# Sums of weight blocks for the seven-product chunks: made between the attention heads and fetched, instead of made in the last stretch

## The chip, the cores and the metric

One core of one Trainium2 chip runs the whole program. The metric is device time in microseconds (us). The kernel before has a median of 1070.12 us over three runs (1069.92 to 1073.11). A difference of about 0.3% is what a measurement of this kernel can tell from none.

## What is computed

Block-causal attention for 8 batches of 8 heads (576 positions, head width 64), then a feed-forward layer on the 4608 tokens of 512 features, with a hidden width of 2048:

```python
scores = 0.125 * q @ k.T                       # per head, 576 x 576
scores = where(row // 64 >= col // 64, scores, -1e9)
attn = exp(scores - max) / (sum + 1e-9)
x = (attn @ v)                                 # heads side by side: 4608 x 512
h = x @ w_in                                   # 512 x 2048
g = maximum(0.01 * h, h)
out = g @ w_out                                # 2048 x 512
```

Everything is float32. For TensorE each matrix of the feed-forward layer is split into a rounded high part and a low part (what is left after rounding), and a product is made of three: high by high, high by low, low by high.

## The kernel before

**Stages.** The 64 heads are worked through one after another. The first 14 turn their probabilities on TensorE; the other 50 turn them with VectorE transposes (L795) and two trips through DRAM (`way`, `turn`). The tokens make 18 chunks of 256. Twelve of them go through the plain feed-forward code, `ffn1` (L894) and `ffn2` (L921), whose matmuls stand between those of the heads and behind them. The last six chunks go through `tail()` as three pairs, and the tail is what the change is about.

**The tail.** A pair of chunks is multiplied with seven block products where eight would be needed: each matrix is cut into 2 by 2 blocks, sums and differences of blocks are multiplied, and the results are combined. For each of the eight units `u` of the hidden width, `first8` (L1092) makes seven products of `x` and `w_in` blocks with six matmuls each, VectorE combines them out of PSUM (L1105), ScalarE applies the leaky ramp (L1108), and the result is stored to DRAM in `gd` through four staging buffers, two for even and two for odd units. When the three pairs are through, `second8` (L1221) reads `gd` back and makes seven products with `w_out` blocks in 24 steps.

**The weight sums.** The seven products need sums of weight blocks, high part plus low part, added and subtracted in a fixed way. `combos(u)` makes those of `w_in`: one operation on 128x512 and six on 128x256 into scratch (`xin` for the first seven units, the unused `x8` for the eighth), then a split of the four results into high and low parts in `sum8[u]` and in place of one weight block. This lies ahead of the first pair. `combos2(u)` makes those of `w_out`: two operations on 128x512 and four on 128x256 in the scratch `x8`, a split of one result over a weight block, and a store of the other three to DRAM in `td`. These eight pieces stand among the products of `first8`, at the places listed in `SUMS`. `combos3(u)` fetches `td` into `sum8[u]` once `first8` of the third pair is done with unit `u`, and splits it. The additions go through `op2`, which offers each to VectorE (L965) and to GpSimd (L966).

**What sets the order.** `Plan` walks through a model of the five engines and writes one fixed order per engine; each operation has a rank (its due place, in heads, or from 1000 on in the tail) and a choice of engines with costs. Operations of VectorE named `DVE+` and all of GpSimd are not planned to run at the same time; those named `DVE` may run beside GpSimd. The plan only sets orders: at run time nothing keeps the two engines apart. All DMAs are issued by SyncE in one order, so an issue that waits holds back those behind it. `split_x` and `splits8` split the inputs; `inputs8` loads a pair's inputs into `x8` (1024 KB).

Of the kernel before, what the change touches and what calls it, by code (L numbers as in the profile page):

```python
# [9 lines left out]
F32 = mybir.dt.float32  # L10
# [26 lines left out]
RL = -2.684  # L37
# [14 lines left out]
SUMS = [1, 2, 4, 10, 11, 12, 14, 19]  # L52
EARLY = 7
RL8 = -6.0
RT8 = -1.0
RM = 11.035
# [3 lines left out]
RS = -16.177  # L60
RG = -8.8
OFF1 = 3.882
# [11 lines left out]
FILLTO = -153.36  # L74
# [206 lines left out]
def attention_ffn(ctx: ExitStack, tc: tile.TileContext, q2: bass.AP, k2: bass.AP, qk: bass.AP, v: bass.AP, w_in: bass.AP, w_out: bass.AP, out: bass.AP):  # L281
# [84 lines left out]
    td = fixed([P, 3 * CH], F32, "td", NU, dram)  # L366
# [416 lines left out]
    def turn(i, row, pkeys):  # L783
# [22 lines left out]
        flipped(0, 13, 14, 1, 0, 0, 64)  # L806
        for y, (a0, a1, b0, b1) in enumerate(((0, 1, 1, 4), (1, 3, 0, 4), (3, 4, 0, 3))):
# [131 lines left out]

    def tail():  # L940
        if not TAIL:
            return
# [9 lines left out]
        old += [("xh", 1, e) for e in cells]  # L952
# [8 lines left out]

        def op2(n, dst, one, two, plus, rank, reads, writes, by=None):
            name = "tensor_add" if plus else "tensor_sub"
            both = [
                ("DVE", dve2(n), lambda: getattr(nc.vector, name)(dst(), one(), two())),  # L965
                ("POOL", pool2(n), lambda: getattr(nc.gpsimd, name)(dst(), one(), two())),  # L966
            ]
            add(both[1:] if by == "POOL" else both, rank, reads, writes)
# [17 lines left out]

        def combos(u, rank):
            w0, w1 = wkeys[("wi", u)], wkeys[("wi", u + NU)]
            s0, s1 = [("S", u, 0)], [("S", u, 1)]
            heap, keys = (flat8, x8s) if u >= EARLY else (raw8, xins)  # L990
            at = lambda y, n=1: heap()[:, y * CH : (y + n) * CH]
            four = lambda ap: ap.rearrange("p (d f) -> p d f", f=P)
            op2(WIDE, lambda: four(at(1, 2)), lambda: f32(sides(u, 0)), lambda: f32(sides(u, 1)), True, rank, w0, keys)
            for h in range(2):
                op2(
                    CH, lambda h=h: four(at(3 * h)), lambda h=h: f32(sides(u + NU, 0)[:, 2 * h : 2 * h + 2]),
                    lambda h=h: f32(sides(u + NU, 1)[:, 2 * h : 2 * h + 2]), True, rank, w1, keys,
                )
            op2(CH, lambda: at(3), lambda: at(0), lambda: at(3), True, rank, [], keys)
            op2(CH, lambda: at(0), lambda: at(1), lambda: at(0), False, rank, [], keys)  # L1000
            op2(CH, lambda: at(1), lambda: at(3), lambda: at(1), False, rank, [], keys)
            op2(CH, lambda: at(2), lambda: at(2), lambda: at(1), False, rank, [], keys)
            split(3 * CH, lambda: sum8(u, 0), lambda: sum8(u, 1), lambda: at(1, 3), rank, keys, s0, s1)
            split(
                CH, lambda: sides(u + NU, 0)[:, 0:2], lambda: sides(u + NU, 1)[:, 0:2], lambda: four(at(0)), rank, keys,
                [x for x in w1 if not x[1]], [x for x in w1 if x[1]],
            )

        def combos2(u, rank):
            w0, w1 = wkeys[("wo", u)], wkeys[("wo", u + NU)]  # L1010
            base = 4 * (u % 2)
            at = lambda y, n=1: flat8()[:, (base + y) * CH : (base + y + n) * CH]
            d8 = 2 * (u % 2)
            c0, c1, c2, c3 = (in8(d8 + d, d8 + d + 1, h * CH, (h + 1) * CH) for d in range(2) for h in range(2))
            for y, (f, w) in enumerate(((u, w0), (u + NU, w1))):
                op2(WIDE, lambda y=y: at(2 * y, 2), lambda f=f: f32(woh[:, f]), lambda f=f: f32(wol[:, f]), True, rank, w, (c2 + c3) if y else (c0 + c1))
            op2(CH, lambda: at(0), lambda: at(1), lambda: at(0), False, rank, c1, c0)
            op2(CH, lambda: at(1), lambda: at(3), lambda: at(1), False, rank, c3, c1)
            op2(CH, lambda: at(3), lambda: at(3), lambda: at(0), False, rank, c0, c3)
            op2(CH, lambda: at(2), lambda: at(3), lambda: at(2), False, rank, c3, c2)  # L1020
            split(
                CH, lambda: woh[:, u, CH:], lambda: wol[:, u, CH:], lambda: at(0), rank, c0,
                [x for x in w0 if not x[1]], [x for x in w0 if x[1]],
            )
            add([("SP", ISSUE, lambda: nc.sync.dma_start(td[u], at(1, 3)))], rank, c1 + c2 + c3, [("td", u)], lag="gs")

        def combos3(u, rank):
            s0, s1 = ("S", u, 0), ("S", u, 1)
# [328 lines left out]
```

## Time and profile before

| | us |
|---|---|
| median of three runs (lowest, highest) | 1070.12 (1069.92, 1073.11) |
| profiled execution, its own time | 1071.98 |
| its span in the trace | 1070.2 |
| TensorE busy | 1027.7 |
| VectorE busy | 798.8 |
| ScalarE busy | 610.5 |
| GpSimd busy | 420.1 |

The table of stretches gives the busy time of each engine in a window; where TensorE's busy time equals the window, it never stood still for longer than its pipeline hides. The table of waits names, for the engine's idle time, who ended it. A matmul's duration in the trace contains its pipeline, so matmuls overlap and their mean durations don't add up to busy time. In the tables `x` is the tile `x8`, `sum` is `sum8`, `more` and `piles` and the upper half of `xin` are the staging buffers, `p_s`, `p_v`, `p_h`, `p_o` are PSUM tiles, and `big` and `new` hold the split inputs.

### The profile page before, as it was taken

What the parts mean: (1) busy time and instruction counts of PE and PEld (TensorE: products, weight loads), DVE (VectorE), ACT (ScalarE), POOL (GpSimd) and SP (SyncE); (2) the same over time, 40 slices, a digit from 0 to 9 for tenths busy, and PEclk for the clock granted to TensorE, in tenths of its full rate; (3) what the DMA queues carried; (4) which work ended last, traced back from release to release, by engine and by line L of the source; (5) the groups of instructions that cost most, each with busy time, mean ns of one, the idle gap of its engine ahead of it and who ended that gap; (6) DMA issues with size and microseconds to landing.
All of it is one profiled execution on the core that took longest, in us unless ns stands there. A gap on an engine that the chain in (4) does not pass through costs nothing. (4 is left out here: it accounts for less than half of the span.)

```text
span 1070.2 us, 21248 instructions
## 1 busy us (share of the span) xinstructions
PE 1027.7 (96%) x7336; PEld 910.8 (85%) x7336; DVE 798.8 (75%) x1932; ACT 610.5 (57%) x1437; POOL 420.1 (39%) x413
## 2 busy tenths in 40 slices
PE   7979999999999999999999999999999789889998
PEld 4658889888888888888888888888999789879998
DVE  7887978688778787878768778760998767578664
ACT  7778768576766665666756656651443434434332
POOL 3344227253343444345433423421435534155331
PEclk9999999999999999999999999999999999999999
DMA  6554534676776576786766865574005466665442
GB/s 202 164 185 137 167 106 132 208 211 178 222 207 211 182 224 179 216 242 173 231 200 201 226 177 178 169 232 118 21 10 169 139 206 182 190 194 172 150 155 72
DMA packets 131228, 185.80 MB, mean 174 GB/s; under 512 B 14896, under 2 KB 103728, under 8 KB 131120
## 3 DMA queue, kind: packets, MB, share of 16 engines
q1 hardware_dynamic: 131120, 184.44, 57.3%
q8 instruction: 58, 0.95, 0.4%
q14 instruction: 50, 0.41, 0.1%
HBM read 107.68 MB, written 76.71 MB: 172 GB/s over the span
## 5 line engine op out<-in xcount | busy, mean ns | idle before, releaser
L894 PE MATMUL p_h<-big,wih 128*128 128x256 f32 x1216 | 246.7, 281 | 0.0
L921 PE MATMUL p_o<-woh,big 128*128 128x512 f32 x768 | 236.8, 395 | 0.0
L894 PEld LDWEIGHTS p_h<-big,wih 128*128 128x128 f32 x1216 | 200.0, 189 | 10.0 <-issue 2.2
L312 POOL TENSOR_TENSOR big<-piles,big 128x512 fp32r<-128x512 f32 x80 | 106.3, 1329 | 204.0 <-ACT big L297 169.6
L795 DVE STREAM_TRANSPOSE turn<-prow 128x128 f32<-128x128 f32 (+3 forms) x400 | 144.8, 396 | 21.5 <-POOL prow L630 5.4
L921 PEld LDWEIGHTS p_o<-woh,big 128*128 128x128 f32 x768 | 133.3, 188 | 21.4 <-issue 2.4
L630 POOL TENSOR_SCALAR prow<-prow,nmrec 128x448 f32<-128x448 f32 (+4 forms) x98 | 60.3, 621 | 176.0 <-DVE nmrec L617 134.3
L894 PE MATMUL p_h<-big,wil 128*128 128x256 f32 x448 | 123.4, 280 | 0.0
L921 PE MATMUL p_o<-wol,big 128*128 128x512 f32 x384 | 119.7, 393 | 0.0
L909 ACT ACTIVATE piles<-p_h 128x512 f32<-128x512 f32 x96 | 57.2, 596 | 87.9 <-PE p_h L894 83.3
L600 ACT ACTIVATE prow<-p_s,nmrec 128x448 f32<-128x448 f32 (+4 forms) x150 | 83.1, 559 | 32.3 <-DVE nmrec L591 27.1
L894 PE MATMUL p_h<-xh,wih 128*128 128x256 f32 x320 | 87.8, 280 | 0.0
L894 PE MATMUL p_h<-xh,wil 128*128 128x256 f32 x320 | 87.3, 278 | 0.0
L921 PEld LDWEIGHTS p_o<-wol,big 128*128 128x128 f32 x384 | 72.2, 188 | 15.7
L894 PEld LDWEIGHTS p_h<-big,wil 128*128 128x128 f32 x448 | 85.2, 190 | 0.3
L600 ACT ACTIVATE prow<-p_v,nmrec 128x576 f32<-128x576 f32 (+1 forms) x150 | 71.4, 484 | 19.1 <-DVE nmrec L591 18.5
L312 POOL TENSOR_TENSOR ks<-qk_in,ks 64x576 fp32r<-64x576 f32 x52 | 74.5, 1433 | 5.1 <-DMA turn<-way 1.5
L710 PE MATMUL p_v<-turn,vt 128*64 128x256 f32 (+3 forms) x700 | 75.7, 368 | 0.0
L591 DVE TENSOR_REDUCE nmrec<-p_s 128x1 f32<-128x448 f32 (+4 forms) x150 | 72.0, 518 | 1.1
L710 PEld LDWEIGHTS p_v<-turn,vt 128*64 128x64 f32 x700 | 44.5, 137 | 28.6 <-issue 17.9
L632 ACT ACTIVATE prow<-prow,nmrec 128x320 f32<-128x320 f32 (+4 forms) x113 | 59.0, 536 | 12.4 <-DVE nmrec L617 12.1
L297 ACT CAST ks<-qk_in 64x576 fp32r<-64x576 f32 x63 | 42.3, 671 | 36.7 <-PE p_v L570 30.7
(281 smaller groups left out, 2376.5 us busy)
## 6 DMA issues: line engine op xcount, KB each, us to landing
way<-turn SPq DMA_DIRECT2D x50, 448.0 KB, 3.8
way<-turn SPq DMA_DIRECT2D x100, 168.0 KB, 3.5
turn<-way SPq DMA_DIRECT2D x100, 168.0 KB, 3.6
qk_in<-in_qk SPq DMA_DIRECT2D x50, 288.0 KB, 3.8
turn<-way SPq DMA_DIRECT2D x100, 112.0 KB, 3.6
out<-piles SPq DMA_DIRECT2D x36, 256.0 KB, 3.4
raw<-in_w_in SPq DMA_DIRECT2D x16, 512.0 KB, 4.0
raw<-in_w_out SPq DMA_DIRECT2D x16, 512.0 KB, 3.7
```

Source lines behind the costliest of these rows:

```text
L297: one = lambda: nc.scalar.copy(dst(), src())
L312: ("POOL", pool2(n), lambda: nc.gpsimd.tensor_sub(dst(), one(), two())),
L591: [("DVE", dve(kw[t]), lambda t=t, ap=ap, flat=flat: nc.vector.tensor_reduce(nm[z][: qn[t], at_col[t] : at_col[t] + 1], ap[: qn[t]], axis= ...
L600: nc.scalar.activation(o, ap[: qn[t]], AF.Exp, bias=nm[z][: qn[t], at_col[t] : at_col[t] + 1], scale=1.0, accum_out=sums[z][: qn[t], at_co ...
L630: ("POOL", pool1(kw[t]), lambda: nc.gpsimd.tensor_scalar(p(), p(), by, 1.0, op0=ALU.mult, op1=ALU.mult)),
L632: ("ACT", act(kw[t], True) + 108, lambda: nc.scalar.mul(p(), p(), by)),
L710: nc.tensor.matmul(dst, later["vt"][z][:, j], src, start=start, stop=stop)
L795: nc.vector.transpose(dst, src.rearrange("p (s b i) -> p s b i", b=4, i=32))
L894: nc.tensor.matmul(p_h[z][:, i, :], w[:, d, f * P : (f + 1) * P], (xl if x else xh[y])[:, d, :], start=first and k == 0 and (u > 0 or i == ...
L909: add([("ACT", act(512), lambda: nc.scalar.activation(g, p_h[z], AF.Prelu, alpha=0.01))], rank, [("h", z)], ["g"])
L921: nc.tensor.matmul(p_o[m], a[:, i, m * P : (m + 1) * P], w[:, u + NU * i, :], start=u == 0 and k == 0, stop=u == NU - 1 and k == 5,)
```

## The change

The sums of `w_in` and of `w_out` are both made by a new function, `sums_ahead`, in 16 pieces (two for each unit) with ranks 22.0, 24.136, and so on to 54.04, that is, among the heads from the 23rd on. Each piece waits for the transposes of the head of its rank. The scratch is `xr`, which held the first batch's attention output until the third plain chunk had read it; it is cut in two halves, one for `w_in` pieces and one for `w_out` pieces. All additions of these pieces are given to VectorE (`PREBY`). At the end of each piece SyncE stores four results (512 KB) to DRAM in `td`, which grows from three to eight blocks for each unit. In the tail, `brought` takes the place of the additions: it loads one block or three blocks from `td` into the low part's place, ScalarE or VectorE rounds them into the high part's, and a subtraction leaves the low part. `op2`'s VectorE choice is now named `DVE+`. The pace of three plain chunks, and numbers that place loads, the splits and the trips through DRAM, are changed too.

```diff
-RL = -2.684
+RL = -2.305
-RX = -0.204
+RX = -0.49
-PACE = [5.0, 5.0, 5.67, 4.14, 5.0, 5.0, 4.52, 5.0, 5.0, 5.0, 5.0, 5.17, 5.0, 5.0, 5.0, 5.0, 6.28, 4.59]
+PACE = [5.0, 5.0, 5.67, 4.14, 5.46, 5.0, 4.52, 5.0, 5.55, 5.39, 5.0, 5.17, 5.0, 5.0, 5.0, 5.0, 6.28, 4.59]
-SUMS = [1, 2, 4, 10, 11, 12, 14, 19]
-EARLY = 7
+SUM0 = 2
+RC8 = -8.0
+PRE0 = 22.0
+PRE1 = 2.136
+PREBY = "DVE"
...
+    def sums_ahead():
+        spare = [("spare", y, c) for y in range(2) for c in range(4)]
+        add([("POOL", 1, lambda: None)], 0, [], [("x", 0, h, y) for h in range(H) for y in range(2)] + spare)
...
+            rank = PRE0 + PRE1 * j
+            gate = [("head", min(int(rank), NH - 1))]
...
+                sum_of(WIDE, lambda: four(at(1, 2)), lambda: side(u, 0), lambda: side(u, 1), True, rank, w0 + gate, k1 + k2)
...
+                sum_of(CH, lambda: at(2), lambda: at(3), lambda: at(2), False, rank, k3, k2)
+            add([("SP", ISSUE, lambda: nc.sync.dma_start(td[u][:, y], at(0, 4)))], rank, k0 + k1 + k2 + k3, [("td", u, y)], lag="pre")
...
-                ("DVE", dve2(n), lambda: getattr(nc.vector, name)(dst(), one(), two())),
+            ("DVE+", dve2(n), lambda: getattr(nc.vector, name)(dst(), one(), two())),
...
+        def brought(u, y, rank, part, top, low, tops, lows):
+            a, e = (0, 1) if part else (1, 4)
+            src = lambda: td[u][:, y, a * CH : e * CH]
...
+            add([("SP", ISSUE, lambda: nc.sync.dma_start(f32(low()), shape(src())))], rank + RC8, [("td", u, y)], lows, lag="in1" if part else "in3")
+            n = (e - a) * CH
+            casting(n, top, lambda: f32(low()), rank, lows, tops)
+            op2(n, low, lambda: f32(low()), lambda: f32(top()), False, rank, tops, lows)
```

Up to the first of the new additions the orders of VectorE and TensorE are those of before, row by row apart from buffer numbers: VectorE's first 493 rows and TensorE's first 1151. From there they differ. Three places show how.

VectorE among the heads, about the 37th head, in the changed kernel: `nmrec` and `prow` are the heads' maxima and probabilities, `turn` the transposed ones, `xr` the scratch of the sums.

```order
L594 TENSOR_REDUCE nmrec<-p_s 128x1 x2
L798 STREAM_TRANSPOSE turn_1489<-prow_0_111 64x4x32
L947 TENSOR_TENSOR xr<-woh,wol 128x512
L544 SCALAR_TENSOR_TENSOR qs_1471<-qk_in,qs_1471 64x576
L619 TENSOR_REDUCE nmrec<-sums 128x3
L620 RECIPROCAL nmrec<-nmrec 128x3
L947 TENSOR_TENSOR xr<-woh,wol 128x512
L634 TENSOR_SCALAR prow_1_112<-prow_1_112,nmrec 128x192
L634 TENSOR_SCALAR prow_0_111<-prow_0_111,nmrec 64x64
L947 TENSOR_TENSOR xr<-xr 128x256
L619 TENSOR_REDUCE nmrec<-sums 128x2
```

The additions stand one by one between the steps of the heads, all on VectorE; before, nothing of `xr` or of the weights stood there.

VectorE in the tail, where the third unit of the first pair is combined, in the kernel before:

```order
L1105 TENSOR_TENSOR xin<-more,p_h_689 128x2x128
L965 TENSOR_TENSOR x_8058<-x_8058 128x256
L1105 TENSOR_TENSOR xin<-xin,p_h_690 128x2x128
L965 TENSOR_TENSOR x_8058<-x_8058 128x256
L1105 TENSOR_TENSOR xin<-xin,p_o_100 128x2x128
L965 TENSOR_TENSOR x_8058<-x_8058 128x256
L965 TENSOR_TENSOR wol<-x_8058,woh 128x256
L965 TENSOR_TENSOR x_8058<-x_8058 128x256
L1105 TENSOR_TENSOR more<-more,p_h_690 128x2x128
L1105 TENSOR_TENSOR piles<-piles,p_s 128x2x128
L965 TENSOR_TENSOR x_8058<-x_8058 128x256
```

And in the changed kernel, from the second unit of the first pair on:

```order
L947 TENSOR_TENSOR x_8287<-x_8287 128x2x256
L1123 TENSOR_TENSOR piles<-piles,p_s 128x2x128
L947 TENSOR_TENSOR xin<-x_8287 128x512
L1123 TENSOR_TENSOR more<-more,p_v 128x2x128
L1123 TENSOR_TENSOR xin<-more,p_h_689 128x2x128
L1123 TENSOR_TENSOR xin<-xin,p_h_690 128x2x128
L1123 TENSOR_TENSOR xin<-xin,p_o_100 128x2x128
L1123 TENSOR_TENSOR more<-more,p_h_690 128x2x128
L1123 TENSOR_TENSOR piles<-piles,p_s 128x2x128 x2
L1123 TENSOR_TENSOR piles<-piles,p_v 128x2x128 x3
```

The combining steps now follow each other; the two differences of the next pair's inputs (`x`, `xin`) stand behind the 9th combining step of the pair, where before they stood behind the 33rd, since `x8` is no longer scratch.

SyncE's issues at the end of the first pair's stores (`gd_80`) and the start of the second pair's (`gd_81`), in the changed kernel:

```order
L1155 DMA gd_80<-more 128x2x128
L1155 DMA gd_80<-piles 128x4x128 x2
L1155 DMA gd_80<-more 128x2x128
L1059 DMA x_8287<-xt_97 128x4x512
L1155 DMA gd_81<-more 128x4x128
L1155 DMA gd_81<-xin 128x4x128
L1155 DMA gd_81<-more 128x2x128
L1155 DMA gd_81<-piles 128x4x128 x2
```

Before, the third pair's load of inputs (the row with `xt`) stood among the stores of the second pair's fourth unit, and eight stores to `td` stood among the `gd` stores of the three pairs; now the load opens the second pair and no store to `td` is among them.

SyncE among the heads in the changed kernel, at the store of one piece:

```order
L815 DMA way_72<-turn_1492 32x1344
L986 DMA td_87<-xr 128x1024
L531 DMA qk_in<-in_qk 128x576
L827 DMA turn_1492<-way_72 32x3x448
L827 DMA turn_1492<-way_72 32x448
```

The new store stands ahead of the next head's inputs and of a trip back from DRAM.

## Rows read from the trace of the kernel before

**Rows 1.** The page's first part: busy us, share of the span, instructions

```profile
PE 1027.7 (96%) x7336; PEld 910.8 (85%) x7336; DVE 798.8 (75%) x1932; ACT 610.5 (57%) x1437; POOL 420.1 (39%) x413
```

**Rows 2.** Stretches of the whole: length, busy us (instructions) by engine, clock, DMA share, GB/s

```profile
0.00:50.00 50.00, 40.44 (x260) 29.29 (x261) 38.59 (x113) 37.68 (x104) 19.79 (x36) 1.00 0.64 195
50.00:100.00 50.00, 43.89 (x295) 33.27 (x294) 41.13 (x104) 38.83 (x101) 20.26 (x16) 0.93 0.49 147
...
233.00:496.00 263.00, 263.00 (x1823) 228.65 (x1822) 206.06 (x583) 171.89 (x432) 108.17 (x108) 1.00 0.69 202
...
711.00:800.00 89.00, 89.00 (x589) 78.52 (x588) 53.90 (x100) 33.00 (x63) 27.23 (x20) 1.00 0.23 69
```

**Rows 3.** Stretches of the tail's first products, 800 to 941, same columns

```profile
840.00:860.00 20.00, 15.41 (x121) 14.33 (x120) 18.44 (x28) 8.01 (x20) 16.14 (x14) 1.00 0.45 144
...
sum 141.00, PE 123.45 PEld 119.29 DVE 100.52 ACT 56.24 POOL 60.46; mean PE 17.64 PEld 17.04 DVE 14.36 ACT 8.04 POOL 8.64
```

**Rows 4.** Waits of TensorE, 800 to 941: total us, times, longest us

```profile
PE p_v L1092 <- DVE piles L1105: 4.0, 3, 2.0
PE p_v L1092 <- DVE more L1105: 2.4, 2, 1.9
PE p_v L1221 <- ACT piles L1108: 2.1, 1, 2.1
PE p_h L1092 <- DVE piles L1105: 1.7, 1, 1.7
PE p_h L1092 <- DVE big L965: 1.3, 1, 1.3
PE p_s L1092 <- ACT piles L1108: 1.2, 1, 1.2
PE p_v L1092 <- ACT piles L297: 1.2, 1, 1.2
```

**Rows 5.** Additions in scratch, 800 to 941, by shape: busy us, mean ns, idle before

```profile
L965 DVE TENSOR_TENSOR x<-x 128x256 f32<-128x256 f32 x28 | 19.2, 687 | 0.0
L965 DVE TENSOR_TENSOR x<-woh,wol 128x512 f32<-128x512 f32 x6 | 6.4, 1072 | 1.0 <-DMA td<-x 1.0
L965 DVE TENSOR_TENSOR x<-wih,wil 128x256 f32<-128x256 f32 x2 | 0.8, 419 | 0.0
L965 DVE TENSOR_TENSOR x<-wih,wil 128x512 f32<-128x512 f32 x1 | 0.7, 684 | 0.0
...
L966 POOL TENSOR_TENSOR x<-woh,wol 128x512 f32<-128x512 f32 x10 | 15.8, 1591 | 2.8 <-DMA td<-x 2.0 <-DVE big L965 0.6
L966 POOL TENSOR_TENSOR x<-x 128x256 f32<-128x256 f32 x11 | 9.3, 844 | 5.4 <-DMA x<-gd 3.4 <-DVE x L965 1.7
```

**Rows 6.** Line 965 between 750 and 800: duration ns min/median/max, first and last start

```profile
L965 DVE TENSOR_TENSOR xin<-xin x27: 424/426/1398, 752.7 to 792.0; 128x256 f32<-128x256 f32 x27
```

**Rows 7.** DMA issues by tile, 800 to 941: times, KB each, median us to landing

```profile
gd<-piles SPq DMA_DIRECT2D x23, 256.0 KB, 2.5
...
x<-xt SPq DMA_DIRECT2D x1, 1024.0 KB, 8.9
```

**Rows 8.** ScalarE's instructions around 838, 875, 882: start, us, [idle before <- releaser]

```profile
837.87 0.37 ACT L297 COPY piles<-p_v 128x256 f32<-128x256 f32 x1 [4.39 <-DMA gd<-piles]
...
874.66 0.37 ACT L297 COPY piles<-p_s 128x256 f32<-128x256 f32 x1 [1.44 <-DMA gd<-piles]
...
881.86 0.37 ACT L297 COPY more<-p_o 128x256 f32<-128x256 f32 x1 [3.50 <-DMA gd<-more]
```

**Rows 9.** VectorE's transposes of heads 22 (first) and 55 (last): start, us

```profile
232.63 0.90 DVE L795 STREAM_TRANSPOSE turn<-prow 128x384 f32<-128x384 f32 x2 [0.70 <-POOL prow L630]
...
495.38 0.77 DVE L795 STREAM_TRANSPOSE turn<-prow 128x384 f32<-128x384 f32 x2 [0.17 <-ACT prow L632]
```

**Rows 10.** GpSimd's subtractions for the plain chunks, 233 to 496, and VectorE's longest wait there

```profile
L312 POOL TENSOR_TENSOR big<-piles,big 128x512 fp32r<-128x512 f32 x32 | 42.2, 1319 | 76.3 <-ACT big L297 59.7 <-DVE big L298 15.3 <-POOL prow L630 0.8
...
DVE p_v L318 <- PE p_v L570: 18.1, 19, 2.4
```

**Rows 11.** The heads' last matmuls on `turn`: duration ns, first and last start us

```profile
L710 PE MATMUL p_v<-turn,vt x56: 272/327/644, 720.5 to 738.7; 128*64 128x128 f32 x16, 128*64 128x256 f32 x16, 128*64 128x192 f32 x16, 128*64 128x512 f32 x8
```

More of the change, by code (lines that the diff above doesn't have):

```diff
@@ L806, in turn @@
         flipped(0, 13, 14, 1, 0, 0, 64)
+        plan.writer["head", i] = plan.writer["turn", x, 0, 0]
         for y, (a0, a1, b0, b1) in enumerate(((0, 1, 1, 4), (1, 3, 0, 4), (3, 4, 0, 3))):
@@ L938, in ffn2, with op2 @@
                 add([("SP", ISSUE, store)], rank, [key], [("out", c, m)], lag="out")
+    def op2(n, dst, one, two, plus, rank, reads, writes, by=None):
+        name = "tensor_add" if plus else "tensor_sub"
+        both = [
+            ("DVE+", dve2(n), lambda: getattr(nc.vector, name)(dst(), one(), two())),
+            ("POOL", pool2(n), lambda: getattr(nc.gpsimd, name)(dst(), one(), two())),
+        ]
+        add(both[1:] if by == "POOL" else both[:1] if by == "DVE" else both, rank, reads, writes)
@@ L951, in tail @@
         old += [("x", 0, h, y) for h in range(H) for y in range(2)] + [("xs", d, y) for d in range(2) for y in range(2)]
-        old += [("xh", 1, e) for e in cells]
+        old += [("xh", 1, e) for e in cells] + [("spare", y, c) for y in range(2) for c in range(4)]
         in8 = lambda d0=0, d1=ND, e0=0, e1=2 * CH: [("x8", d, e) for d in range(d0, d1) for e in range(e0, e1, BLK)]
@@ L985, in sum8 @@
             return later["sum8"][u][:, low].rearrange("p a b -> p (a b)")
-        def combos(u, rank):
[L988 to L1005, printed above, removed]
@@ L1009, in combos2 @@
         def combos2(u, rank):
[L1010 to L1025, printed above, removed]
-        def combos3(u, rank):
-            s0, s1 = ("S", u, 0), ("S", u, 1)
-            add([("SP", ISSUE, lambda: nc.sync.dma_start(f32(sum8(u, 1)), td[u]))], rank, [("td", u)], [s1], lag="gs")
-            rank = max(rank, TR + 8 * TAIL + u // 2 + RT8)
-            casting(3 * CH, lambda: sum8(u, 0), lambda: f32(sum8(u, 1)), rank, [s1], [s0])
-            op2(3 * CH, lambda: sum8(u, 1), lambda: f32(sum8(u, 1)), lambda: f32(sum8(u, 0)), False, rank, [s0], [s1])
+            w0 = wkeys[("wo", u)]
+            brought(u, 1, rank, 1, lambda: woh[:, u, CH:], lambda: wol[:, u, CH:], [x for x in w0 if not x[1]], [x for x in w0 if x[1]])
+        def combos3(u, rank):
+            brought(u, 1, rank, 0, lambda: sum8(u, 0), lambda: sum8(u, 1), [("S", u, 0)], [("S", u, 1)])
         def inputs8(k, rank):
@@ L1271, in tail @@
                 first8(k, u, TR + 8 * k + u)
-                for y in range(NU):
-                    if int(SUMS[y]) == 8 * k + u:
-                        combos2(y, TR + SUMS[y])
+                y = 8 * k + u - SUM0
+                if y >= 0 and y % 2 == 0 and y // 2 < NU:
+                    combos2(y // 2, TR + 8 * k + u)
                 if k == TAIL - 1:
-                    combos3(u, TR + 8 * k + u)
+                    combos3(u, TR + 8 * TAIL + u // 2 + RT8)
         for n in range(8 * TAIL):
@@ L1319, in attention_ffn @@
                 ffn2(c, u, rank + rate[c] * LAG / NU + 0.003)
-    tail()
+    if TAIL:
+        sums_ahead()
+        tail()
     if FILL:
```

58 lines of the change are left out of this document (40 added, 18 removed), and 2 rows, old and new, of the table MOVES.

## The prediction

> **What bounds the kernel now.** I read the busy times first [rows 1]: TensorE is busy 96% of the span, the next engine, VectorE, 75%. The average hides the stages, so the stretches come next [rows 2]. From 0 to 100 us TensorE is idle for 9.6 + 6.1 = 15.7 us while the program starts. From 233 to 496 it is busy for all 263 us, and for all 89 us from 711 to 800: TensorE alone sets the time there, and work on other engines is free as long as TensorE finds its operands. In the tail's first products, 800 to 941, it is busy 123.45 of 141 us [rows 3]: 17.5 us are lost, most densely between 840 and 860, where VectorE is busy 18.44 of 20 us and GpSimd 16.14. TensorE's waits there [rows 4] name the releasers: the seven rows make 13.9 us, the other seven of that table, each 0.8 or less, make 3.6. Nearly all wait for VectorE to empty a PSUM bank (L1105) or for ScalarE.
>
> I sort the 17.5 us by their roots. ScalarE's copies into the staging buffers at 838, 875 and 882 stand behind stores to `gd` that have not landed [rows 8]. A store of 256 KB lands in 2.5 us in the median, but the 1024 KB load of the next pair's inputs, issued on the same queue, takes 8.9 us [rows 7], and the stores behind it share its time. The waits of 1.2 us (L297), of 2.0 (the longest of the first row) and of 1.7 fall at these copies: **4.9 us come from DMA**. Of what VectorE released (4.0 + 2.4 + 1.7 + 1.3 and 2.9 of the small ones = 12.3) the other **8.6 us come from VectorE being late**, since additions in the scratch stand between its combining steps. The remaining 4.0 us, among them 2.1 for the first step of `second8`, wait for ScalarE.
>
> **What the change removes.** The additions of rows 5 go: 19.2 + 6.4 + 0.8 + 0.7 = 27.1 us of VectorE's 100.5 and 15.8 + 9.3 = 25.1 of GpSimd's 60.5 (a few of these belong to `second8` and stay). Two things follow. VectorE's share in this stretch falls from 71% to 52%. And what stays gets shorter where both engines ran at once: an addition of 128x256 takes 0.426 us in the median and up to 1.398 [rows 6], and 0.687 in the mean in the tail, where GpSimd is busy, against 0.419 where it isn't [rows 5]. Of the 8.6 us I take three quarters as gone, 6.4 us; a quarter stays because seven splits of the next pair's inputs still fall on the last unit of the pair before, whose operands they overwrite (the 1.3 us of `big` [rows 4] is such a wait). The bounds are 0 and 8.6.
>
> The 4.9 us of DMA: the second pair's load is now issued before the first pair's first store, so the wait at 838 (1.2) goes. The third pair's load now opens the second pair. It still has stores behind it, but the 384 KB stores to `td` that stood among them are gone: of the 2.0 + 1.7 us I take half, 1.8, as gone. Something comes back. A load is freed by the last split of its pair, and the order puts only eight combining steps, a unit and a third, between that split and the difference that reads the load. A unit takes TensorE 123.45 / 24 = 5.1 us [rows 3], so the load has 6.9 us and takes up to 8.9 [rows 7]; VectorE would wait 2 us there, with combining steps queued behind, in two pairs. With the stores to `td` gone the load should be quicker; I take 1 us for each pair. DMA's part of the gain is 1.2 + 1.8 - 2.0 = 1.0 us, between -4.0 and 4.9. The 4.0 us behind ScalarE and the hand-over to `second8` stay: the fetches of the second half and their splits stand there as before. **Gain in the tail: 6.4 + 1.0 = 7.4 us, between -4.0 and 12.6 with the 4.0 us behind ScalarE kept, 17.5 without.**
>
> **What it adds.** (1) 16 pieces on VectorE: eight with one addition of 128x512 and six of 128x256, eight with two and four, so 24 and 80. Without GpSimd beside them: 24 x 0.684 + 80 x 0.419 = 49.9 us; with it, at the means of the tail: 24 x 1.072 + 80 x 0.687 = 80.7 us [rows 5]. Counting eight transposes a head, they lie between 233 and 496 us [rows 9], where VectorE is busy 206.06 of 263 and so idle for 56.9 us [rows 2]. The low price fits, with 7 us over; the high one doesn't. I take the low end, because GpSimd is busy there 108 of 263 us (41%) against 16.14 of 20 where the high prices come from, and because 18.1 us of the idle time is VectorE waiting for TensorE to finish scores [rows 10], which means that it is early, not late. So I cost them at nothing: TensorE's own work covers them. If that cover is gone, the next head's scores wait for a PSUM bank that VectorE hasn't read, and each us that VectorE is behind is a us of TensorE.
>
> (2) 16 stores of 512 KB, and the waits that they bring: SyncE holds each until the last addition, with the next head's `qk_in` and the trip back of a `turn` queued behind it; those who wait are TensorE's score and value matmuls. Added bytes there are 8 MB in 263 us, 32 GB/s on 202 [rows 2]. The same orders carry DMAs of up to 448 KB for each head now without a wait of TensorE; I cost them at nothing, and at most at the price of (1).
>
> (3) 16 loads of 128 KB and 16 of 384 KB in the place of eight stores and eight loads. The first half (4 MB, and 1 MB of the second) can start when the heads' memory is free, after 739 us [rows 11], and has to 796 us; at the 202 GB/s of rows 2 that is 25 us. It fits, and the DMA share there is 0.23. The splits behind them cost what those behind the additions cost before.
>
> (4) The new pace and places: the program's start, and with it the 15.7 us, is the same row by row up to the first addition. After it TensorE never idled before, so another order can only lose there; I take nothing, with the bound in the second rival.
>
> **Sum.** The profiled execution's span is 1070.2 us and its own time 1071.98; the median of the runs is 1070.12, so a us of the span counts as one of the median. 1070.1 - 7.4 = **1062.7 us**.
>
> **Where the Trainium skill speaks against it.** VectorE and GpSimd slow each other when both read from SBUF: rows 6 shows 0.426 against 1.398 us, and GpSimd's subtraction takes 1.319 us in the mean among the heads [rows 10]. The Trainium skill (SBUF — State Buffer, "Who interferes with whom") says that a VectorE instruction with two SBUF inputs contends with a GpSimd instruction that reads SBUF, and that the second to come is fully blocked until the first ends. By that rule no planned order protects the sums, since the order binds each engine alone, and they would delay the plain chunks' subtractions on GpSimd too. The trace agrees with the blocking. What it would cost here is the second rival, which is worked out from rows alone.
>
> **Rivals.**
> *All of it.* If the whole 17.5 us goes, as TensorE's full windows elsewhere suggest it may: 1070.1 - 17.5 = 1052.6. For it: most TensorE waits end within 2 us, and VectorE at 52% has room. Against: the load of 8.9 us and the splits at the pair's change stay. 12%.
>
> *VectorE late among the heads (slower).* If the additions meet GpSimd's work as in the tail, they take 80.7 us in 56.9 us of room: 23.8 us late, all of it TensorE's, since one PSUM bank per score tile leaves it nothing to do first: 1062.7 + 23.8 = 1086.5. It turns the sign once an addition takes more than (56.9 + 7.4) / 104 = 0.62 us in the mean, where the low price is 0.48 and the high one 0.78. For it: idle time of an engine that works in a fixed order is not free to be moved, and GpSimd works 41% of the time. Against: from 711 to 800 the same additions ran on VectorE beside GpSimd's subtractions and TensorE lost nothing [rows 2]. 16%.
>
> *The stores set the pace.* The change takes VectorE's part away, but TensorE then waits for the staging buffers, whose stores were late by 4.39, 1.44 and 3.50 us [rows 8]: the 6.4 us come back as waits for `gd`, and what is left is DMA's 1.0: 1070.1 - 1.0 = 1069.1, no change by what can be told. For it: three of the larger waits are DMA's. Against: all eight `td` stores that pressed on them in the queue are gone. 11%.
>
> *It doesn't do what it says.* The fetched blocks come too late and the first products wait for them. Each us late is a us of TensorE; with 25 us of transfer in 57, 5%, and then around 1070.
>
> **How the numbers follow.** The forecast has 56%. Faster by over 0.3% (under 1066.9; 0.3% is what a measurement of this kernel can tell) are the forecast's case and the first rival, 0.68. Within 0.3% (to 1073.3): the third, most of the fourth, 0.15. Slower: the second and the rest, 0.17. The range runs from 1053, where the first rival stands, to 1072, past the third and fourth; what is left out is most of the second rival and the tip of the first, under 2 in 10.
>
> **What would show it.** Right: TensorE busy for the whole of 233 to 496 with VectorE above 95% of it; additions at L947 on `xr` near 0.48 us in the mean; the tail's first products with some 10 us of idle TensorE, and its waits for `piles` and `more` at L1123 at a third; the tail starting at 796 as before. Wrong: waits of TensorE among the heads, on `p_s`, `p_v` or `turn`, which would be the second rival; ScalarE's copies waiting for `gd` for longer than before, the third; waits for `sum` or `wil` on `td`, the fourth.

## The result and the profile after

The changed kernel takes 1054.98 us (median of four runs, 1052.72 to 1055.86) against 1070.18 beside it: ratio 0.9849, 95% interval 0.9825 to 0.9872, so 15.2 us faster. Forecast were 7.4 us. The direction was right and the time lies in the range (1053 to 1072), but the gain is twice what the sum gave. A second timing of the same kernel gave 1056.38 us beside 1071.9, ratio 0.9853 [0.9831, 0.9875].

The page's first part, then stretches of the whole (columns as in [rows 1, 2]):

```profile
PE 1021.6 (97%) x7336; PEld 906.6 (86%) x7336; DVE 792.4 (75%) x2000; ACT 609.8 (58%) x1435; POOL 353.1 (34%) x347
```

```profile
50.00:100.00 50.00, 43.51 (x319) 33.16 (x318) 43.60 (x106) 40.36 (x105) 22.39 (x18) 1.00 0.53 161
233.00:496.00 263.00, 263.00 (x1818) 229.53 (x1817) 222.21 (x616) 167.82 (x417) 109.89 (x104) 1.00 0.70 213
711.00:800.00 89.00, 89.00 (x605) 78.11 (x604) 44.49 (x102) 40.08 (x87) 15.67 (x14) 1.00 0.49 156
...
820.00:840.00 20.00, 20.00 (x172) 20.00 (x172) 11.37 (x26) 8.84 (x20) 4.28 (x6) 1.00 0.43 132
800.00:941.00 141.00, 133.62 (x1124) 131.27 (x1123) 82.54 (x170) 61.90 (x126) 30.10 (x32) 1.00 0.61 179
```

Among the heads TensorE is busy for all 263 us as before, with VectorE at 84%. In the tail's first products GpSimd's work is halved against [rows 3] and VectorE's is 18 us less. The row of 820 to 840 is what a stretch without loss looks like: 172 matmuls in 20 us, 0.1163 us each. The whole stretch in the kernel before, for comparison:

```profile
800.00:941.00 141.00, 123.45 (x1010) 119.29 (x1009) 100.52 (x193) 56.24 (x126) 60.46 (x57) 1.00 0.59 180
```

By that pace the 1010 matmuls of the window need 117.5 of the 141 us, so 23.5 us were lost, not the 17.5 that busy time shows; after, 1124 need 130.7 and 10.3 are lost.

TensorE's waits from 800 to 941 after, the whole table (total us, times, longest):

```profile
PE p_v L1110 <- ACT more L300: 2.0, 1, 2.0
PE p_s L1239 <- ACT new L300: 1.0, 1, 1.0
PE p_s L1239 <- DVE big L947: 1.0, 1, 1.0
PE p_o L1110 <- ACT more L300: 1.0, 1, 1.0
PE p_o L1110 <- ACT piles L300: 0.8, 1, 0.8
PE p_s L1239 <- ACT big L300: 0.7, 1, 0.7
PE p_v L1110 <- DVE piles L1123: 0.4, 2, 0.2
PE p_s L1239 <- DVE new L947: 0.3, 1, 0.3
PE p_v L1110 <- DVE more L1123: 0.2, 1, 0.2
```

Of VectorE's part of [rows 4] 0.6 us are left in the first products (L1110). What is left there waits for ScalarE's copies into the staging buffers.

From here on "first products" is the time from the start of the first matmul of `first8` to the end of its last, worked out from the trace of each kernel: 144.6 us before (795.6 to 940.2), 128.7 after (793.7 to 922.4). The traces' spans differ by 19.3 us, more than the medians, since the trace of before is of a run 1.9 us above its median and that of after 2.3 below: 15.9 of first products, 1.4 behind them, 1.9 ahead. The last is chance: TensorE's granted clock fell to 0.5 (1.2 GHz) for some 3.4 us at a time in the first 100 us, twice in the profiled execution of before [rows 2], never in this one, three stretches' worth in a third, of the same changed kernel, whose tail began at 797.5.

### The profile page after: what moved, and what is told of

Same layout as the page of the kernel before. It is cut to its first block, busy times and chain, and to the rows that moved or that the text cites. A ratio compares the mean times of both kernels' runs of the same rounds, so it can differ in the third digit from the quotient of the medians.

```text
span 1050.9 us, 21285 instructions
## 1 busy us (share of the span) xinstructions
PE 1021.6 (97%) x7336; PEld 906.6 (86%) x7336; DVE 792.4 (75%) x2000; ACT 609.8 (58%) x1435; POOL 353.1 (34%) x347
## 4 chain that ended last, share of the span: by engine, by line
PE 91%; DMA 4%; DVE 2%; ACT 2%; issue 0%; SPq 0%; DVEq 0%; ACTq 0%
PE p_h L898 26%; PE p_o L925 25%; PE p_v L713 7%; PE p_v L573 4%; PE p_s L573 3%; PE p_h L1239 3%; PE p_s L1239 3%; PE p_o L1239 2%; PE p_v L1110 2%; PE p_s L562 2%; PE p_s L1110 2%; PE p_v L1239 2%; PE p_h L1110 2%; PE p_o L1110 2%; PE p_v L668 2%; PE p_v L757 1%
## 5 line engine op out<-in xcount | busy, mean ns | idle before, releaser
L633 POOL TENSOR_SCALAR prow<-prow,nmrec 128x448 f32<-128x448 f32 (+4 forms) x89 | 54.4, 618 | 121.2 <-DVE nmrec L620 103.1
L315 POOL TENSOR_TENSOR ks<-qk_in,ks 64x576 fp32r<-64x576 f32 x57 | 81.7, 1433 | 17.9 <-ACT ks L300 11.9
L635 ACT ACTIVATE prow<-prow,nmrec 128x192 f32<-128x192 f32 (+4 forms) x112 | 59.3, 550 | 11.3 <-DVE nmrec L620 10.8
```

The source lines that it names most:

```text
L315: ("POOL", pool2(n), lambda: nc.gpsimd.tensor_sub(dst(), one(), two())),
L635: ("ACT", act(kw[t], True) + 108, lambda: nc.scalar.mul(p(), p(), by)),
```

## The experiments

All times are medians; the kernel before beside them took 1070.6 to 1072.1 us. "Back" means that the operations run and nobody reads what they make. The planner makes a new order for every edit, so that a run shows its edit together with the order that comes of it.

### The DMA side alone, and the additions alone

**e2**: the `td` stores back in the changed kernel, fed from a weight block.

```diff
+                        add([("SP", ISSUE, lambda y=y, src=src: nc.sync.dma_start(tx[y], src()))], TR + SUMS[y], [("gd", k, u, 0), ...], [("tx", y)], lag="gs")
```

> The changed kernel with eight stores of 384 KB that nobody reads added at the eight old places of the td stores; no additions come with them. Theory A (additions): 0 to 2 us slower, 1055 to 1057. Theory B (DMA): 6 us or more slower, above 1061, with ScalarE's copies waiting for gd as long as in the kernel before.

1057.07 us, 2.1 us slower, first products 129.3 us. The stores alone, which wait for no addition here, are not the cause.

**f1**: the additions back.

```diff
+            key = ["xa"]
+            for f in (u, u + NU):
+                opd(WIDE, lambda: at(0, 2), lambda f=f: f32(woh[:, f]), lambda f=f: f32(wol[:, f]), True, rank, wkeys[("wo", f)], key)
+            for y in range(4):
+                opd(CH, lambda y=y: at(y % 2), lambda: at(1), lambda: at(0), False, rank, [], key)
```

> The changed kernel (1055.0 us) with the eight sets of w_out additions back at their old places among the first products, offered to VectorE and GpSimd as before, into the lower half of xin; nobody reads their results and nothing is stored. Theory A (the gain is the additions leaving the tail, and it is larger than forecast because busy time hides part of each stall): 9 to 14 us slower than the changed kernel, 1064 to 1069. Theory B (the gain is the DMA side): under 4 us slower. The run with the td stores back, 2.7 us slower with a tail of 129.3 us against 128.7, already speaks against B.

1055.53 us, first products 126.7. My own theory fell here: VectorE carries the additions again and TensorE loses nothing:

```profile
800.00:941.00 141.00, 133.72 (x1115) 131.44 (x1115) 98.15 (x203) 62.10 (x130) 45.48 (x48) 0.98 0.61 181
```

VectorE is as full as before (98.15 against 100.52 us), TensorE as busy as after.

### One part taken from the kernel before

**f2** leaves out the additions, **f3** moves the stores ahead, **h1** does both.

```diff
-                op2(WIDE, lambda y=y: at(2 * y, 2), lambda f=f: f32(woh[:, f]), lambda f=f: f32(wol[:, f]), True, rank, w, (c2 + c3) if y else (c0 + c1))
-            op2(CH, lambda: at(0), lambda: at(1), lambda: at(0), False, rank, c1, c0)
...
-            add([("SP", ISSUE, lambda: nc.sync.dma_start(td[u], at(1, 3)))], rank, c1 + c2 + c3, [("td", u)], lag="gs")
```

> The kernel before (1070.2 us) with the eight sets of w_out additions left out of the tail; the splits and the td stores stay where they are and use what the scratch holds, so this leaves out part of the computation. No sums are made among the heads. Theory A: 10 to 15 us faster than before, 1055 to 1060, with the first products at about 130 us in place of 144.6. My forecast's sizing (6.4 us from VectorE): 1063 to 1065. Theory B: within 4 us of before.

> The kernel before with the eight td stores moved out of the first products to a place ahead of the tail, where they store weight blocks instead of sums (so the last sums are wrong); all additions stay in the tail. Theory A: within 3 us of before. Theory B: 5 us or more faster. My forecast put 1.0 us on the DMA side as a whole, 4.9 at most.

> The kernel before (1070 to 1072 us) with the eight sets of w_out additions left out and the eight td stores moved ahead of the tail, where they store weight blocks: part of the computation is left out. No sums among the heads. Taken singly, leaving out the additions gave 12.0 us of first products and leaving out the stores 11.1; added up that would be 23, which is more than there was to lose. If they are one chain (a store that waits at the head of SyncE's queue for a late addition, with the gd stores behind it), the second adds little to the first: first products of 127 to 131 us, 14 to 17 less than before's 144.6. If they were two separate costs, under 124. The w_in sums stay ahead of the tail here, so what is left to the changed kernel's 128.7 is their part: my reckoning 0 to 2 us.

First products 132.6 (f2), 133.5 (f3) and 131.5 us (h1), against 144.6. So 12.0 and 11.1 us singly, and 13.1 together: either one takes nearly all. The two could have added: by the pace of a full stretch the 1008 matmuls of the first products need 117.2 us, so 27.4 us were lost there. The text ahead of h1 says that 23 is more than there was to lose; it isn't. Counted from the first products to the end of the program, f2 gains 11.9, f3 10.1 and h1 10.6 us. The medians are 1059.01, 1066.13 and 1064.10; f3 (4.7 us faster, between what theories A and B gave) and h1 lose time elsewhere: their stores now run at the start of the program, and TensorE is busy 131.04 and 129.14 of the 133 us from 100 to 233.

The edits also move the load of the next pair's inputs into `x8`: the third pair's leaves at 846.7 in f2, at 864.8 in f3 and at 850.4 in h1, in the kernel before at 870.95. Of the 15.9 us, 2.8 are left to the rest of the change (sums of `w_in`, fetches, places). In h1's trace one stall of TensorE, 3.0 us at 860.0, is as large; VectorE, whose combining step ends it, had waited for that load (in f2 the same happens, 2.1 us):

```profile
856.44 0.69 DVE L965 TENSOR_TENSOR x<-x 128x512 f32<-128x512 f32 x1 [2.71 <-DMA x<-xt]
```

### Both back, with and without the tie

**g4** has additions and stores back, each store behind its additions and out of their scratch; **l1** has the same additions, with stores of weight blocks, so that neither waits for the other.

```diff
+            add([("SP", ISSUE, lambda: nc.sync.dma_start(tx[u][:, : 2 * CH], at(0, 2)))], rank, key, [("tx", u, 0)], lag="gs")
```

> The changed kernel with additions (lower half of xin) and the td-like stores both back and unused, each store behind its additions, and the load left early. Theory D: within 4 us of the changed kernel, first products under 132 us. Theory E: 6 us or more slower, above 1061.

> The changed kernel with the unused additions (as in f1) and eight unused stores of 384 KB (as in e2) both back, but with no tie between them: the stores take weight blocks, so no store waits for an addition and no addition for a store. With the tie (g4) the same operations cost 9 us and 7.1 us of first products, and a set of additions there waits 3.3 us for the store before it to land. If the tie is what costs: 0 to 3 us slower than the changed kernel, 1055 to 1058, first products under 131 us. If it is enough that both are there: 6 us or more slower, above 1061.

g4: 1064.48 us, first products 135.8. l1: 1058.49, 0.5 above the range given for it, first products 126.5. The work of l1 is all there and costs the first products nothing; it is 3.5 us slower by a single wait of 7.4 us behind them, at 931.6, for a ScalarE copy, and whether the work or the new order brings that wait isn't shown. **The tie, with the order planned for it, costs more than the work**: 6.0 us in the medians and 9.3 in the first products lie between l1 and g4. In g4 all sets share one scratch, in the kernel before they have two by turns, so its tie is the tighter one. g4's trace shows where. GpSimd, SyncE, VectorE, ScalarE and again GpSimd in turn (start, us, [idle before <- releaser]):

```profile
864.97 1.32 POOL L958 TENSOR_TENSOR xin<-woh,wol 128x512 f32<-128x512 f32 x1 [3.32 <-DMA tx<-xin]
```

```profile
876.25 2.16 SPq L1175 DMA_DIRECT2D gd<-more  x2
881.22 0.33 SPq L1069 DMA_DIRECT2D tx<-xin  x1
881.60 0.42 SPq L1070 DMA_DIRECT2D tx<-woh  x1
882.12 1.00 SPq L1175 DMA_DIRECT2D gd<-piles  x2
```

```profile
877.36 0.41 DVE L1143 TENSOR_TENSOR piles<-piles,p_h 128x256 f32<-128x256 f32 x1
877.69 0.63 DVE L957 TENSOR_TENSOR xin<-xin 128x256 f32<-128x256 f32 x1
878.24 0.41 DVE L1143 TENSOR_TENSOR piles<-piles,p_o 128x256 f32<-128x256 f32 x1
878.57 1.18 DVE L957 TENSOR_TENSOR xin<-xin 128x256 f32<-128x256 f32 x1
879.68 0.41 DVE L1143 TENSOR_TENSOR piles<-piles,p_o 128x256 f32<-128x256 f32 x1
880.01 1.19 DVE L957 TENSOR_TENSOR xin<-xin 128x256 f32<-128x256 f32 x1
881.11 0.41 DVE L1143 TENSOR_TENSOR piles<-piles,p_o 128x256 f32<-128x256 f32 x1
```

```profile
881.68 0.42 ACT L1146 ACTIVATE piles<-piles 128x256 f32<-128x256 f32 x1
884.08 0.62 ACT L301 CAST new<-xin 128x512 fp32r<-128x512 f32 x1 [1.98 <-DVE xin L949]
885.59 0.37 ACT L301 COPY piles<-p_h 128x256 f32<-128x256 f32 x1 [0.90 <-DMA gd<-piles]
```

```profile
877.99 2.91 POOL L950 TENSOR_TENSOR big<-x,big 128x512 fp32r<-128x512 f32 x2
```

A set can't start before the store of the one ahead has landed, and that store waits at SyncE for its additions and among the `gd` stores. The second pair's four sets begin at 842.8, 854.3, 865.0 and 874.4, where f1 has them at 844.8, 852.0, 858.0 and 864.2: the last is pushed onto the change of pair. VectorE doesn't wait before it; the order, planned with the tie, puts it there. Two of its additions, beside GpSimd's splits, take 1.18 and 1.19 us between combining steps. The last step ends at 881.5, the ramp at 882.1, the `gd` stores leave at 882.1 and 882.6, the later one lands at 885.5, and the copy that empties `p_h` starts at 885.59: TensorE stands still for 4.2 us until 886.0. The tied store ahead in the queue had left by then and held the `gd` stores for less than a microsecond; the combining steps were late. In the kernel before the staging copies wait for `gd` too [rows 8], both engines wait for a store to free the scratch, and SyncE waits for additions at its `td` stores (L1025; total us, times, longest):

```profile
857.71 0.69 DVE L965 TENSOR_TENSOR x<-woh,wol 128x512 f32<-128x512 f32 x1 [0.97 <-DMA td<-x]
...
857.75 1.83 POOL L966 TENSOR_TENSOR x<-woh,wol 128x512 f32<-128x512 f32 x1 [0.94 <-DMA td<-x]
860.61 1.43 POOL L966 TENSOR_TENSOR x<-woh,wol 128x512 f32<-128x512 f32 x1 [1.02 <-DMA td<-x]
```

```profile
SPq L1025 <- DVE x L965: 2.1, 2, 1.3
SPq L1025 <- POOL x L966: 1.9, 2, 1.2
```

So each link of a ring (addition, store, scratch, addition) shows, and none of these waits is long. That the 11 to 12 us of f2 and f3 run through it follows from the two not adding and from g4 beside l1; no trace shows it stall by stall. Two of the larger stalls of before, 2.0 us at 875.6 and 1.7 at 881.0, follow the third pair's load, which takes 8.9 us among `td` and `gd` stores [rows 7]; in f3, without the `td` stores, it takes 5.3.

### The load's place, and the old stretch put back

**g1** holds back the second and third pair's loads to their old places; **g2** has the additions of f1 besides; **g3** has additions and stores out of `x8` as well.

```diff
+                late = [("gd", k - 1, 4 if k == 1 else 3, 0)] if k else []
-                add([("SP", ISSUE, load)], rank - 50, [("xt", b, y) for y in range(ND)], ...)
+                add([("SP", ISSUE, load)], rank - 50, [("xt", b, y) for y in range(ND)] + late, ...)
```

> The changed kernel (1055.0 us, first products 128.7 us in its trace) with only the load of the second and third pair's inputs held back to the place it had before: behind the stores of the fifth unit of the first pair and of the fourth unit of the second. No additions and no td stores come back. So far: additions back alone cost 0.5 us, td stores back alone 2.7, and from the kernel before each of the two taken away alone gave 12 us of first products, so neither alone is the cause. Theory D (x8 was both scratch and input buffer, which held the load back and pushed the splits into a lump that met other work): 4 to 10 us slower, 1059 to 1065. Theory E (the load's place is hidden, additions and stores act on each other): within 2 us.

> As the one before, with the unused additions also back, in the lower half of xin. Theory D: as slow as or slower than the late load alone, 1062 to 1069, with VectorE and GpSimd full in the ten us after a pair's change. Theory E: within 2 us of the changed kernel. If additions only cost where the splits are late, this run minus the late load alone is their price: over 4 us.

> The changed kernel with all three of the old stretch's features back and unused: the additions in x8, eight td-like stores of 384 KB out of x8, and the load in its old place. If these are the whole of the cause, the first products come back to 140 to 147 us and the time to 1065 to 1071. Under 1060 it would be something else, such as the place of the w_in sums ahead of the stretch.

g1: 1052.59 us, first products 126.4. g2: 1053.63 and 126.9. g3: 1064.53 and 133.8. In the changed kernel the load's old place costs nothing, with the additions or without (theory D falls). g3 brings back 5.1 of the 15.9 us of first products and 9.5 of 15.2 in the median; its trace is of the fastest of six runs, 3.8 us under the median, so that the 5.1 are rather low. **h2** asked whether the rest lay in ScalarE's copies that waited for the additions:

```diff
-                CH, lambda: woh[:, u, CH:], lambda: wol[:, u, CH:], lambda: at(0), rank, c0,
+                CH, lambda: woh[:, u, CH:], lambda: wol[:, u, CH:], lambda: f32(wol[:, u, CH:]), rank, [x for x in w0 if x[1]],
```

> The kernel before with one tie loosened: the w_out block that each set splits over its weight block (a ScalarE or VectorE copy and a subtraction) is taken from the low weight block instead of from the additions' result, so that no copy waits for the additions; additions and td stores stay as they are. The values are then not those wanted. In the trace of before ScalarE waits 6.4 us for the additions at these copies. If that tie carries part of the chain (the old additions and stores put back into the changed kernel gave only 133.8 us of first products, not 144.6): 4 to 8 us faster than before, 1063 to 1067. If not: within 2 us of before.

1069.78 us, ratio 0.9989 [0.9974, 1.0003], first products 142.6: no part that can be told.

### The exclusion by name

**e4** puts `DVE+` into the kernel before, **f4** takes it from the changed kernel.

```diff
-            ("DVE+", dve2(n), lambda: getattr(nc.vector, name)(dst(), one(), two())),
+            ("DVE", dve2(n), lambda: getattr(nc.vector, name)(dst(), one(), two())),
```

> The kernel before with one word changed: op2's VectorE choice is planned as excluding GpSimd (DVE+). Additions stay in the tail. Theory A: within 3 us of before, since the same operations stand on the same two engines and TensorE still waits for VectorE. Theory C (the gain is that VectorE and GpSimd no longer block each other in SBUF, which the naming alone brings): 5 us or more faster, below 1065, with the mean of an addition of 128x256 in the tail falling from 0.69 towards 0.43 us.

> The changed kernel with op2's VectorE choice planned as free to run beside GpSimd (DVE in place of DVE+), which touches the sums among the heads, the splits and the last stretch. Theory A (the place of the additions counts): within 3 us of the changed kernel. Theory C (planning the two engines apart brings the gain): 5 us or more slower. In the kernel before, the same word alone made it 6.9 us slower, so C can hold only where the sums are elsewhere.

e4: 1078.74 us, ratio 1.0073 [1.0051, 1.0095]; an addition of 128x256 took 0.495 us in the mean in place of 0.687 [rows 5], and it was slower all the same (first products 153.7), which neither theory has. Planned apart, VectorE gets 13 of the 16 additions of 128x512, in the kernel before 6. f4: 1116.20 us, ratio 1.0407 [1.0379, 1.0436], 61 us slower than the changed kernel. Its loss is not in the tail (first products 130.8) but among the heads:

```profile
233.00:496.00 263.00, 243.41 (x1616) 206.54 (x1614) 232.41 (x606) 159.82 (x408) 132.79 (x125) 0.95 0.70 214
496.00:711.00 215.00, 199.37 (x1312) 169.11 (x1313) 176.12 (x483) 131.22 (x335) 98.88 (x101) 0.93 0.69 212
```

TensorE is idle for 35.2 of these 478 us, in every other kernel for less than 2, and its clock stood at 1.2 GHz for 54.6 us in four stretches between 466 and 538. The additions from 233 to 496, in the changed kernel and in f4 (busy us, mean ns):

```profile
L947 DVE TENSOR_TENSOR xr<-xr 128x256 f32<-128x256 f32 x40 | 18.2, 455 | 0.1
```

```profile
L947 DVE TENSOR_TENSOR xr<-xr 128x256 f32<-128x256 f32 x40 | 26.1, 653 | 0.2
```

By their starts and ends 20 of the 104 additions meet an instruction of GpSimd in the changed kernel, 70 in f4; all shapes together take 0.51 against 0.72 us in the mean. An addition of 128x256 that meets none takes 0.40 and 0.41 us in the mean, 0.43 at most; one that does, 0.65 and 0.80, up to 1.39 and 1.51.

But f4 doesn't price that alone. The planner gives GpSimd 431 instructions in place of 347 (from 233 to 496 125 in place of 104, each 1.07 us in the mean against 1.06), and what TensorE waits for from 233 to 711 is mostly GpSimd's `ks` and ScalarE's `prow`, and VectorE for less (total us, times, longest):

```profile
PE p_s L573 <- POOL ks L315: 10.3, 5, 4.0
PE p_s L573 <- ACT prow L603: 8.6, 2, 5.9
PE p_v L573 <- DVE xs L694: 4.8, 4, 1.6
```

### What the sums among the heads cost

**e3** adds them to the kernel before, **h3** leaves the additions out of the changed kernel.

```diff
         def sum_of(*args):
-            op2(*args, by=PREBY)
+            pass
```

> The kernel before (median 1070.2 us) with the 16 new pieces among the heads as the change has them, stored to a DRAM tile that nobody reads; its tail keeps its own additions. It prices the added side alone. My reckoning (costed at nothing, covered by TensorE): within 2 us of before, 1068 to 1072, TensorE busy for all 263 us from 233 to 496. The rival (the additions meet GpSimd's and VectorE falls behind): 1075 or more, with waits of TensorE among the heads.

> The changed kernel with the 104 additions among the heads left out; the 16 stores and all that follows stay, and store what the scratch holds. It prices the additions among the heads. I costed them at nothing: within 2 us of the changed kernel's 1055.0. The rival of the prediction (they make VectorE late): 4 us or more faster, below 1051.

e3: 1086.59 us, 14.8 slower, where I had reckoned with 2 at most. Its TensorE is busy for all 263 us among the heads; it loses 2.8 us from 496 to 800 and 12.9 in the first products (157.5), where `combos` now stands behind a VectorE with 58.05 us of work in 711 to 800 in place of 53.90, and the first unit takes 14.1 us, 7.7 before; that the one brings the other is likely and not shown. h3: 1052.18 us, 2.8 faster than the changed kernel, TensorE's 263 us unchanged. So the additions cost 0 to 3 us as the change has them (the intervals of h3 and of the changed kernel overlap), and more if the sums in and ahead of the tail stay.

### A version with the load held back

> The changed kernel as it is, timed again beside the two that follow, on the same chip: 1053 to 1057 us.

> The changed kernel with the loads of the second and third pair's inputs in their old places, timed again in more rounds. In its first run the third unit took 5.1 us in place of 7.2 (no store waits behind the 1024 KB load there) and the first pair 42.6 in place of 44.8; the third pair's late load gave 0.8 of it back. If that is the come-back that my forecast put at 2.0 us, it is 1 to 3 us faster than the changed kernel, 1051 to 1054. If the first run was chance: within 0.5 us.

> Only the second pair's load is held back to its old place; the third pair's stays early. If each load's price lies where the traces show it (2.2 us in the first pair, about 0.8 given back in the second), 2 to 4 us faster than the changed kernel, 1050 to 1053, first products 125 to 127 us. If lateness and earliness cost alike: as the changed kernel, 1053 to 1057.

k1: 1056.38 us, ratio 0.9853. k2 (g1 again): 1054.37, 0.9840 [0.9819, 0.9860]. k3 (one load held back): 1054.94, 0.9844. Held back, the loads are some 2 us better in both timings of it (1052.59 against 1054.98, 1054.37 against 1056.38), less than the intervals tell apart; the 2 to 4 us hoped for from k3 did not come. The traces show where. ScalarE and SyncE in the changed kernel:

```profile
808.79 0.37 ACT L300 COPY more<-p_v 128x256 f32<-128x256 f32 x1 [1.93 <-DMA gd<-more]
```

```profile
800.82 0.98 SPq L1059 DMA_DIRECT2D x<-xt  x2
801.91 0.44 SPq L1155 DMA_DIRECT2D gd<-xin  x1
803.05 1.17 SPq L1155 DMA_DIRECT2D gd<-more  x2
```

The first three stores to `gd` behind the load (two issues, 1024 KB together) land after 6.0, 5.6 and 5.2 us, in g1, where no load is ahead of them, after 2.3, 3.1 and 2.6. The copy waits, and the third unit takes 7.2 us (7.4 in k1); with the load held back 5.1 (g1) and 5.3 (k2, k3).

## Why the prediction was half right

- **What bounds it, and that the sums are free where they went: right.** TensorE kept its 263 us, the additions took 0.51 us in the mean (forecast near 0.48). But I placed all 104 between 233 and 496 and so had VectorE above 95% there. They run from 260 to 645, 65 of them before 496, and VectorE was at 84%: there was more room than I gave them. That it was right rests on the planned order too: in f4 it was not. h3 puts 0 to 3 us on what I costed at nothing.
- **The step that failed is the gain in the tail, 6.4 + 1.0 us, where the first products gave 15.9.** Three things in it were off. The base: busy time gave 17.5 us to lose, the matmuls' pace gives 23.5. The sorting: I gave 8.6 us to VectorE and 4.9 to DMA as two roots and added their gains. The runs show that the two hang together: taking out either the additions or the stores gave 11 to 12 us, both 13.1, and the two put back cost 9.5 us with the tie and 3.5 without. A ring fits this (late addition, store late, scratch and staging buffers held, copy late, combining step late, next addition late), as far as shown above. The share: I kept a quarter of VectorE's part and, of DMA's 4.9, all but 1.0. What VectorE released, 12.3 us of TensorE's waits before, fell to 1.9 in the table above, and ScalarE's waits for `gd` halved (before, then after):

```profile
ACT more L297 <- DMA gd<-more: 11.6, 7, 3.5
ACT piles L297 <- DMA gd<-piles: 7.1, 3, 4.4
...
ACT more L300 <- DMA gd<-more: 4.9, 3, 2.2
ACT piles L300 <- DMA gd<-piles: 4.6, 4, 2.2
```

The sum's upper bound was also added up wrong: 8.6 + 4.9 is 13.5, not 12.6.
- **The come-back of the early load: wrong in place, and right in size by luck.** I put 2.0 us on VectorE's wait for `x8`. VectorE waited 1.0 us, once; the loads landed after 5.9 and 5.1 us. What I overlooked is that in the kernel before it waited for the same two loads longer:

```profile
835.13 0.86 DVE L965 TENSOR_TENSOR x<-x 128x512 f32<-128x512 f32 x1 [1.84 <-DMA x<-xt]
...
879.88 0.69 DVE L965 TENSOR_TENSOR x<-x 128x512 f32<-128x512 f32 x1 [2.92 <-DMA x<-xt]
```

The second stands just ahead of the combining step that ended TensorE's wait of 1.7 us at 881.0. I had put that wait down to the copy at 881.86 [rows 8], which starts later. The price of the early load, some 2 us, was in the third unit, through the `gd` stores behind it.
- **The first rival** (all of it, 12%) came closest, 1052.6 against 1055.0, but by its number alone: it has the whole loss gone, and by the matmuls' pace 10.3 of 23.5 us are still there.
- **The second rival** did not happen, because the order does protect the sums, which I had denied: planned apart, 20 of 104 additions meet GpSimd, and 70 in f4. f4 has that rival's condition and a loss among the heads, though mostly not by its path. At 0.72 us per addition my formula gives 0.72 x 104 - 56.9 = 18 us late; measured were 61. There TensorE waits above all for GpSimd and ScalarE, GpSimd has more to do, and TensorE's clock fell: 35.2 us of idle time and, as an estimate, half of the 54.6 us at half clock make up the 61. The Trainium skill (SBUF — State Buffer, "Who interferes with whom") says that a VectorE instruction with two SBUF inputs contends with a GpSimd instruction that reads SBUF. The durations agree: 0.41 us in the mean for an addition of 128x256 in f4 that meets no GpSimd instruction, 0.80 for one that does. What I drew from it, that no order helps, was mine and wrong.
- **The stores set the pace, and late fetches:** neither shows: ScalarE's waits for `gd` got shorter, and no wait of TensorE in the table above is for `td`.

What stays open: g3 has the ring and not the whole loss (133.8 against 144.6 us of first products), and every edit makes the planner choose engines anew (of 16 additions of 128x512, GpSimd has 10 in before, 9 in g3, 5 in g4, 3 in f1 and l1). How much of the last 11 us is the ring in the old order and how much that choice isn't shown. That copies waited for the additions is excluded as a cause of any size (h2). A late load alone is excluded in the changed kernel (g1); what the load's place is worth among the old additions and stores, nobody has separated: it moved in f2, f3 and h1 as well.

## What to carry to other kernels

Waits that hang together (an engine's result, a store of it in a shared queue, the buffer that the store frees, the same engine again) need not add: here 12.0 and 11.1 us gave 13.1 together. Price them once, and try to cut at the cheapest place. Count lost time of pipelined matmuls by their number and the pace of a full stretch, not by busy time. Two engines that lengthen each other's instructions, as VectorE and GpSimd do here, should be planned apart where work is filled into their idle time among the heads; in the old tail the same word made the kernel 6.9 us slower (e4).

## What the runs showed of the chip

TensorE's clock fell behind a stall: in g4 the stall of 4.2 us that ends at 886.0 is followed by this row, with a granted clock of 0.57, that is mostly 1.2 GHz:

```profile
886.00:890.00 4.00, 3.98 (x20) 3.99 (x21) 3.53 (x4) 1.00 (x2) 2.93 (x2) 0.57 0.17 55
```

It holds 20 matmuls where a full stretch has 34. So that stall cost more than its length, and a slow version can get slower still: 54.6 us at half clock in f4. The third pair's load of 1024 KB landed in 8.9 us among `td` and `gd` stores [rows 7] and in 5.1 at the head of a pair. An addition of 128x256 takes up to 1.51 us beside a GpSimd instruction and at most 0.43 without one.
